# Another rounding of float64 weights, and seven block products for every batch of the second token product

## The chip, the cores and the metric

The kernel runs on one core of a Trainium2 chip. The metric is the device time of one execution in microseconds (us). A core has several engines, each with its own queue of instructions that it works off in order: TensorE (PE in the profile) multiplies matrices into PSUM banks, VectorE (DVE) works element by element, ScalarE (ACT) applies functions and copies, GpSimd (POOL) can add and issues the accumulating DMAs, and SyncE (SP) issues most of the other DMAs. The engines wait for each other through semaphores.

## The reference

Attention with a hash comes first, and a two-layer mixer over tokens and channels follows. The batch is 4, with 8 heads, 768 tokens and a head width of 64, so the model width is 512.

```python
mask = q_bucket[:, :, :, None] == k_bucket[:, :, None, :]      # 6 sign bits of q @ proj, k @ proj
scores = np.where(mask, scale * np.matmul(q, k.transpose(0, 1, 3, 2)), -1000000000.0)
attn = np.exp(scores - np.max(scores, axis=-1, keepdims=True))
attn = attn / (np.sum(attn, axis=-1, keepdims=True) + 1e-09)
x = np.matmul(attn, v)                                         # (4, 768, 512) after the bridge
h = np.maximum(x.transpose(0, 2, 1) @ w_tok1, 0.0) @ w_tok2    # 768 -> 256 -> 768 over tokens
u = x + h.transpose(0, 2, 1)
h2 = np.maximum(u @ w_ch1, 0.0) @ w_ch2                        # 512 -> 1536 -> 512 over channels
out = (u + h2).astype(np.float32)
```

The four weights arrive as float64, the rest as float32. The kernel computes in float32, so it rounds the weights to float32 on the chip.

## The kernel before

There are three stages, each with an order of instructions that is written out by hand.

**Attention** (`attention`) runs over 16 pairs of heads. A round multiplies keys by queries into PSUM (L345), takes the exponential on ACT (L352), adds the exponentials up on DVE (L379 to L386), multiplies them by the values (L397) and divides. The quotient uses the sums of the pair before: ACT takes a logarithm and an exponential (L425, L426), DVE improves the reciprocal (`newton`, L434 and L436), and ACT copies it to other partitions (L442). The result goes to `XT`, in which features lie on partitions and tokens in the rows.

**Conversion** (class `Conversion`) rounds the weights, 768 numbers to each partition at a time. There are 20 such pieces: twelve for `w_tok1`, `w_tok2` and `w_ch1`, spread over the rounds of attention, and eight for `w_ch2` in the token stage. A float64 is two 32-bit words, `lo` and `hi`. `fetch` issues the load on SP (L168). `begin` shifts the high word by three places and puts sign and top bit back (L179, L182). `join` takes the exponent alone as the unit (L194), scales the low word by it (L198) and adds (L199). `end` squares the high word on ACT (L211), so as to set numbers that are too small to zero, and writes the result (L212). `turnover` and `slot` call these steps: in one call of `slot` the last steps of one piece stand ahead of the first steps of the next. In the token stage three raw buffers are used in turn.

**Tokens** (`tokens`) goes over the four batches. `mix1(b)` multiplies by `w_tok1` (L641, 24 records of a matmul for a batch) and applies relu on ACT (L648) into `r1`; after each of its two blocks it runs one entry of a list of jobs. The list's first entry forms sums of channel weights on DVE (L745 to L750), the others are `slot`. `mix2(b, m)` multiplies by `w_tok2` for one half `m` of the features. For batch 0 it makes four blocks of the product with two matmuls each (L690), which ACT copies (L694). For the other batches it makes seven block products in the way of Strassen and Winograd (L698): ACT copies partial results (L703, L706, L708, L710) and five adds make the four blocks (L713 to L717); the second of them (L714) is done by POOL for batches 1 and 2 and by DVE for batch 3. This needs sums of blocks of the left side (`left_sums`, L664 to L667) and of `w_tok2` (`weight_sums`, L618 to L621). A profile counts each of these float32 matmuls as two records. The blocks go to one of three staging places in turn, and POOL adds them to `XT` in memory by an accumulating DMA (`store`, L681). The stage's order: `mix1(b)`, `left_sums(b)`, then both halves of `mix2(b - 1, ...)` with one job between them; `weight_sums` follows in the round of batch 1. At its end stand both halves of batch 3, with sums for the next stage (`inputs`, L594 and L595) between them. Eight PSUM banks are used in turn.

**Channels** (`channels`) multiplies by `w_ch1` and `w_ch2` with nested block products (nearly all of it at L782). It makes up about half of the time.

A second branch recomputes everything in a careful way if a flag is set; with these inputs it isn't entered.

Of the kernel before, what the change touches and what calls it, by code (L numbers as in the profile page):

```python
# [48 lines left out]
def kernel(  # L49
# [83 lines left out]

    NW = 768

    LEAST = float.fromhex("0x1.2p-15")
    double = w_tok1.dtype == I64
    NE = 2 if double else 1

    class Conversion:  # L140


        def __init__(self, pool, parts, bufs, apart=False):
            self.pool, self.bufs, self.apart = pool, bufs, apart
            self.todo = [
                (w, dst, rows, j, n)
                for w, dst, rows, blocks in parts
                for j in range(*blocks, rows)
                for n in range(0, dst.shape[2], NW // rows)
            ]  # L150
            self.fetched, self.begun, self.ready = [], None, None
            for _ in range(bufs - 1):
                self.fetch()
# [17 lines left out]
        def begin(self):  # L171
            if not self.fetched:
                return
            raw, to, rows = self.fetched.pop(0)
            hi = raw[:, :, 1]
            tmp = self.pool.tile([P, 2, NW], F32, name="tmp", tag="cvt", bufs=1)
            big = tmp[:, 0].bitcast(U32)

            nc.vector.tensor_scalar(  # L179
                big, hi, 3, 0x3FFFFFFF, op0=ALU.logical_shift_left, op1=ALU.bitwise_and,  # L180
            )
            nc.vector.scalar_tensor_tensor(  # L182
                big, hi, 0xC0000000, big, op0=ALU.bitwise_and, op1=ALU.bitwise_or,
            )
            self.begun = raw, tmp, to, rows

        def join(self):
            if not self.begun:
                return
            raw, tmp, to, rows = self.begun  # L190
            self.begun = None
            lo, hi = raw[:, :, 0], raw[:, :, 1].bitcast(F32)
            big, unit = tmp[:, 0], tmp[:, 1]
            nc.vector.tensor_scalar(  # L194
                unit.bitcast(U32), big.bitcast(U32), 0xFF800000, None, op0=ALU.bitwise_and,
            )

            nc.vector.scalar_tensor_tensor(unit, lo, 2.0**-52, unit, op0=ALU.mult, op1=ALU.mult)  # L198
            nc.vector.tensor_tensor(big, big, unit, op=ALU.add)  # L199
            self.ready = hi, big, to, rows  # L200

        def end(self):

            if not self.ready:
                return
            size, big, to, rows = self.ready
            self.ready = None
            hi = size
            if self.apart:
                size = self.pool.tile([P, NW], F32, name="size", tag="size", bufs=1)  # L210
            nc.scalar.activation(size, hi, ACT.Square)  # L211
            nc.vector.scalar_tensor_tensor(  # L212
                to, size.rearrange("p (t n) -> p t n", t=rows), LEAST * LEAST,
                big.rearrange("p (t n) -> p t n", t=rows), op0=ALU.is_ge, op1=ALU.mult,
            )

        def turnover(self):

            self.end()
            self.fetch()  # L220
            self.begin()

        def slot(self):

            self.end()
            self.fetch()
            self.begin()
            self.join()

    pairs = [(b, hp) for b in range(B) for hp in range(NP)]  # L230

# [34 lines left out]
    def attention(pool, psum, W1, W2, x0):  # L266
# [202 lines left out]
        for n in range(len(pairs)):  # L469
            halves = [Half(n, half) for half in range(2)]  # L470
            if n:
                load_v(n + 1)
            for now in halves:
                now.scores()
                if n == now.half == 0:
                    hashes(1)
                now.add()
                if now.half == 0:
                    now.add_last()
            if before:  # L480
                before.sums()
            if 0 < n < len(pairs) - 1:
                hashes(n + 1)
            halves[1].add_last()
            if n == 0:
                load_v(1)
            load_qk(n + 2)
            add_values(n)
            if before:
                before.newton()  # L490
            weights.join()
            halves[0].weigh()
            if n + 1 == len(pairs):
                before.divide()
                before = Quotients(halves)
                before.sums()
                before.newton()
                weights.turnover()
                halves[1].weigh()
                break  # L500
            if before:
                before.divide()
            weights.turnover()
            halves[1].weigh()
            if n and n % 2 == 0:
                bounce(pool.tile([P, 2 * S], F32, name="stage", tag="stage", bufs=1), n - 2)
            if n == 2 * NP:
                fetch(0, x0)
            before = Quotients(halves)
# [90 lines left out]
    def tokens(pool, psum, W1, W2, x0, weights, jobs, T, places):  # L600
# [68 lines left out]
        def mix2(b, m):  # L669

            r1, new = R1[b]
            a00, a01, s1, a11 = (
                r1[:, k, P * (2 * m + i) : P * (2 * m + i) + P] for i in range(2) for k in range(2)
            )
            new = new[:, :, P * m : P * m + P]
            ps = [bank("t2")[:, :HALF] for _ in range(4)]
            to = places[(2 * b + m + 1) % 3].rearrange("p (i n t) -> p i n t", i=2, n=2)
            p1, u, p7, p57 = (to[:, i, n] for i in range(2) for n in range(2))

            def store():  # L680
                nc.gpsimd.dma_start(  # L681
                    out=XT[:, 2 * m : 2 * m + 2, S * b : S * b + S], in_=to.rearrange("p i n t -> p i (n t)"),
                    accum_op=ALU.add,
                )

            if not b:
                for n in range(4):
                    for k in range(NJ):
                        at = P * (2 * m + n // 2)
                        nc.tensor.matmul(  # L690
                            ps[n], r1[:, k, at : at + P], W2[:, k, HALF * (n % 2) : HALF * (n % 2) + HALF],
                            start=(k == 0), stop=(k == NJ - 1),
                        )
                    nc.scalar.copy(to[:, n // 2, n % 2], ps[n])  # L694
                return store()

            def product(at, left, right, start=True):
                nc.tensor.matmul(  # L698
                    ps[at], left, right, start=start, stop=True, skip_group_check=True,
                )  # L700

            product(0, a00, b00)
            nc.scalar.copy(p1, ps[0])  # L703
            product(1, a01, b10)
            product(2, s1, sums[:, 0])
            nc.scalar.copy(p57, ps[2])  # L706
            product(3, new[:, 1], b01)
            nc.scalar.copy(p7, ps[3])  # L708
            product(0, new[:, 0], sums[:, 1], False)
            nc.scalar.copy(u, ps[0])  # L710
            product(2, new[:, 2], b11, False)
            product(3, a11, sums[:, 2], False)
            nc.vector.tensor_tensor(p1, ps[1], p1, op=ALU.add)  # L713
            (nc.gpsimd if b + 1 < B else nc.vector).tensor_tensor(p57, p7, p57, op=ALU.add)  # L714
            nc.vector.tensor_tensor(p57, p57, u, op=ALU.add)  # L715
            nc.vector.tensor_tensor(p7, ps[3], u, op=ALU.add)
            nc.vector.tensor_tensor(u, ps[2], u, op=ALU.add)  # L717
            store()

        for b in range(B):  # L720
            mix1(b)
            if b:
                left_sums(b)
                mix2(b - 1, 0)
                job()
                mix2(b - 1, 1)
            if b == 1:
                weight_sums()
        mix2(B - 1, 0)
        inputs(0, T, 0)  # L730
        mix2(B - 1, 1)
# [639 lines left out]
    def attention_and_tokens(W1, W2, x0):  # L1371
# [11 lines left out]
        second["tile"] = second_tile  # L1383

        def weights(pool):
            return Conversion(pool, [(w_ch2, WC2, 3, (0, NHT))], bufs=3, apart=True)

        def jobs(conversion):
            early, late = weight_sums(
                WC1, SW1, slice(0, NCB // 2), slice(NCB // 2, NCB), slice(0, DCH // 2), slice(DCH // 2, DCH),  # L1390
            )
            return [
                lambda: (early(), late()),
                *[conversion.slot] * (NHT * DM // NW + 1),
            ]

        SW2 = second["SW2"].rearrange("p i k c -> p i (k c)")
# [3 lines left out]
    def careful_attention_and_tokens(W1, W2, x0):  # L1401
        def weights(pool, psum):
            conversion = Conversion(pool, [(w_tok1, W1, 3, (0, NR)), (w_tok2, W2, 1, (0, NJ))], bufs=3)
            while conversion.fetched or conversion.ready:
                conversion.slot()

        def turned(pool, psum):
            turn(0, x0, lambda: psum.tile([P, 2, 512], F32, name="trp", tag="tr", bufs=2))
# [58 lines left out]
```

## Time and profile before

Three executions took 805.69, 806.47 and 807.1 us. The profiled one took 806.47 us and has a span of 804.6 us from its first to its last instruction.

| stage | from (us) | to (us) |
|---|---|---|
| start-up and first round of attention | 0 | 27.3 |
| attention, other rounds | 27.3 | 315.65 |
| tokens | 315.65 | 397.24 |
| channels | 397.24 | 795.55 |
| last sums and stores | 795.55 | 804.6 |

Lines such as "L698" point into the kernel before. In a group of instructions "out<-in" are the program's names for what is written and read (`t` is a PSUM bank of the token stage, `second` is memory that holds the staging places and, beside them, converted `w_ch2`, `raw` a loaded float64 piece, `tmp` its working space), followed by the shapes and the count. Durations are in nanoseconds in groups and in microseconds in the time line. A wait names the instruction that waited, then, behind an arrow, the one that ended last before it went on.

### The profile page before, as it was taken

How to read it: one execution, taken by the hardware profiler on the slowest of the kernel's cores; microseconds unless marked ns; L12 is line 12 of the kernel's file. 1: busy time of each engine (PE TensorE's matmuls, PEld its weight loads, DVE VectorE, ACT ScalarE, POOL GpSimd, SP SyncE). 2: the span in 40 equal slices, each digit the busy share in tenths (PEclk: the TensorE clock that was granted, in tenths of full speed). 3: DMA queues.
4: the chain of work that ended last, by engine and by line, in shares of the span. 5: the costliest groups of instructions: out<-in, count | busy, mean ns of one | idle time of the engine just before them, and what ended most of it. 6: DMA issues, size and time to landing. Idle time of an engine off the chain costs nothing.

```text
span 804.6 us, 10632 instructions
## 1 busy us (share of the span) xinstructions
PE 794.9 (99%) x3889; PEld 471.3 (59%) x3889; DVE 672.2 (84%) x884; ACT 441.2 (55%) x707; POOL 57.4 (7%) x80
## 2 busy tenths in 40 slices
PE   9999999999999999999999999999999999999996
PEld 5444444444444444454444458876667886666885
DVE  4789999999999677989867879888769897778986
ACT  5688888888888886243223221237773335775111
POOL 1000000000000000022221010011100012000000
PEclk9999999999999999999999999999999999999999
DMA  4435353537353424886646995499744578630454
GB/s 162 158 121 159 121 160 122 160 121 238 130 165 107 140 61 159 236 248 171 153 79 206 302 355 196 159 282 270 243 141 140 216 211 198 213 110 1 159 180 114
DMA packets 90701, 138.09 MB, mean 172 GB/s; under 512 B 29640, under 2 KB 63376, under 8 KB 88336
## 3 DMA queue, kind: packets, MB, share of 16 engines
q1 hardware_dynamic: 82480, 112.47, 41.9%
q0 software_dynamic: 7456, 24.12, 13.3%
q10 hardware_dynamic: 704, 0.74, 0.3%
q8 instruction: 33, 0.54, 0.3%
q14 instruction: 28, 0.23, 0.1%
HBM read 97.21 MB, written 33.16 MB: 162 GB/s over the span
## 4 chain that ended last, share of the span: by engine, by line
PE 95%; DVE 3%; issue 1%; POOL 0%; ACT 0%; DVEq 0%; POOLq 0%
PE b L782 49%; PE sc L345 20%; PE acc L397 16%; PE t L641 4%; PE sums L421 2%; PE t L690 1%; PE hp L306 1%; PE t L698 1%; PE hw L324 1%; PE idle L459 0%; DVE tmp L179 0%; DVE second L713 0%; DVE second L715 0%; POOL second L714 0%; DVE second L212 0%
## 5 line engine op out<-in xcount | busy, mean ns | idle before, releaser
L352 ACT ACTIVATE e<-sc 128x768 f32<-128x768 f32 x192 | 154.0, 810 | 12.8 <-PE sc L345 12.5
L345 PE MATMUL sc<-qk 64*128 64x384 f32 x768 | 156.7, 487 | 0.0
L782 PE MATMUL b<-R,second 128*128 128x256 f32 (+1 forms) x612 | 150.9, 404 | 0.0
L782 PEld LDWEIGHTS b<-R,second 128*128 128x128 f32 x612 | 116.3, 190 | 31.6 <-issue 17.2
L788 ACT COPY c<-b 128x512 f32<-128x512 f32 (+1 forms) x78 | 37.4, 488 | 169.5 <-PE b L782 155.7
L397 PE MATMUL acc<-e,vn 128*64 128x384 f32 x768 | 127.6, 488 | 0.0
L383 DVE TENSOR_TENSOR esd<-esd,e 128x768 f32<-128x768 f32 x96 | 92.0, 958 | 10.0
L397 PEld LDWEIGHTS acc<-e,vn 128*64 128x64 f32 x768 | 53.6, 137 | 73.1 <-issue 71.8
L345 PEld LDWEIGHTS sc<-qk 64*128 64x128 f32 x768 | 67.5, 187 | 49.3 <-issue 46.4
L782 PE MATMUL b<-XT,WC 128*128 128x256 f32 (+1 forms) x264 | 82.6, 457 | 0.1
L782 PEld LDWEIGHTS b<-XT,WC 128*128 128x128 f32 x264 | 50.1, 190 | 30.1 <-issue 25.1
L345 PE MATMUL sc<-bits 64*128 64x384 bf16 x384 | 62.9, 323 | 0.2 <-DVE bits L328 0.2
L379 DVE SCALAR_TENSOR_TENSOR esd<-e 128x768 f32<-128x768 f32 x32 | 30.3, 948 | 17.6 <-ACT e L352 17.6
L641 PE MATMUL t<-x,W 128*128 128x512 f32 x96 | 41.8, 593 | 0.0
L442 ACT COPY rec<-rec 32x384 f32<-32x384 f32 x64 | 32.6, 509 | 10.1 <-DVE rec L436 9.5
L681 POOL DMA_DIRECT2D XT<-second x8 | 9.9, 1235 | 382.9 <-DVE tmp L198 338.3
L782 PE MATMUL b<-XT,SW 128*128 128x256 f32 (+1 forms) x120 | 34.6, 422 | 0.0
L345 PEld LDWEIGHTS <-bits 64*128 64x128 bf16 x384 | 19.3, 94 | 25.4 <-DVE bits L328 0.8
L782 PE MATMUL b<-TA,WC 128*128 128x512 f32 x72 | 33.8, 592 | 0.0
L782 PE MATMUL b<-TA,SW 128*128 128x512 f32 x72 | 32.9, 592 | 0.0
L403 ACT ACTIVATE num<-acc,vsum 128x384 f32<-128x384 f32 x32 | 18.6, 581 | 24.9 <-PE acc L397 24.5
L386 DVE TENSOR_TENSOR esd<-esd,e 128x768 f32<-128x768 f32 x32 | 30.5, 954 | 1.9
(220 smaller groups left out, 1149.8 us busy)
## 6 DMA issues: line engine op xcount, KB each, us to landing
second<-left SPq DMA_DIRECT2D x18, 1344.0 KB
raw<-in_moe_w_ch SPq DMA_DIRECT2D x16, 768.0 KB
qk<-in_qk SPq DMA_DIRECT2D x15, 768.0 KB
seen<-in_qk POOLq DMA_DIRECT2D x21, 384.0 KB, 3.9
WC<-hidden_left SPq DMA_DIRECT2D x15, 448.0 KB
vn<-in_v SPq DMA_DIRECT2D x16, 384.0 KB
vt<-in_vT SPq DMA_DIRECT2D x16, 384.0 KB
x<-bounced SPq DMA_DIRECT2D x4, 1536.0 KB
```

Source lines behind the costliest of these rows:

```text
L345: nc.tensor.matmul(sc[:, i, :HALF], t[rows, 1, P * c : P * c + P], t[rows, 0, qs], start=start, stop=not start,)
L352: nc.scalar.activation(e, sc[:, :, :HALF], ACT.Exp, scale=SCALE)
L379: nc.vector.scalar_tensor_tensor(self.d, es[0], NR * EPS, es[1], op0=ALU.add, op1=ALU.add,)
L383: nc.vector.tensor_tensor(self.d, self.d, e, op=ALU.add)
L386: nc.vector.tensor_tensor(self.d, self.d, self.es[-1], op=ALU.add)
L397: nc.tensor.matmul(acc[D * i : D * i + D], vn[:, i, c], e[:, i], start=(c == 0), stop=(c == NR - 1),)
L403: nc.scalar.activation(nums[self.n][:, self.half], acc, ACT.Identity, scale=-1.0, bias=vsum,)
L421: nc.tensor.matmul(ps[at : at + 32], ones[:, :32], self.halves[h].d[:, i], start=True, stop=True,)
L442: nc.scalar.copy(rec[other : other + 32, h], rec[at : at + 32, h])
L641: nc.tensor.matmul(ps, W1[:, r, P * j : P * j + P], x[:, r], start=(r == 0), stop=(r == NR - 1),)
L782: nc.tensor.matmul(ps, left(k), right(k), start=start and k == ks[0], stop=stop and k == ks[-1], skip_group_check=True,)
L788: nc.scalar.copy(c, ps)
```

## The change

It has two parts.

*Rounding.* ACT now multiplies the high word, read as a float32, by 2 to the power of minus 112 and takes its absolute value into a buffer `size`; this step is `begin`, and it takes over what the square was for. `join` takes the shifted exponent as the unit, shifts `size` itself in place, scales the low word and adds. `end` puts the sign of the high word back. In attention `begin` moves from `turnover` to the place ahead of `newton`, so a piece is now begun and ended in the same round. In tokens a job is `one`: begin, join, end and fetch of one piece. There is a `size` buffer for each raw buffer but one (one in attention, two in tokens) and one `unit` buffer, in place of `tmp`.

*Second token product.* Batch 0 is now also made by seven block products. So `weight_sums` moves to batch 0's round, ahead of `left_sums`, which now runs for batch 0 too. All five adds are on DVE for every batch.

```diff
         def begin(self):
...
-            hi = raw[:, :, 1]
-            tmp = self.pool.tile([P, 2, NW], F32, name="tmp", tag="cvt", bufs=1)
-            big = tmp[:, 0].bitcast(U32)
-
-            nc.vector.tensor_scalar(
-                big, hi, 3, 0x3FFFFFFF, op0=ALU.logical_shift_left, op1=ALU.bitwise_and,
-            )
-            nc.vector.scalar_tensor_tensor(
-                big, hi, 0xC0000000, big, op0=ALU.bitwise_and, op1=ALU.bitwise_or,
-            )
-            self.begun = raw, tmp, to, rows
+            size = self.pool.tile([P, NW], F32, name="size", tag="size", bufs=self.bufs - 1)
+            nc.scalar.activation(size, raw[:, :, 1].bitcast(F32), ACT.Abs, scale=EXPONENTS)
+            self.begun = raw, size, to, rows
 
         def join(self):
...
             nc.vector.tensor_scalar(
-                unit.bitcast(U32), big.bitcast(U32), 0xFF800000, None, op0=ALU.bitwise_and,
+                unit.bitcast(U32), size.bitcast(U32), 3, 0x7F800000,
+                op0=ALU.logical_shift_left, op1=ALU.bitwise_and,
             )
-
-            nc.vector.scalar_tensor_tensor(unit, lo, 2.0**-52, unit, op0=ALU.mult, op1=ALU.mult)
-            nc.vector.tensor_tensor(big, big, unit, op=ALU.add)
-            self.ready = hi, big, to, rows
+            nc.vector.tensor_scalar(
+                size.bitcast(U32), size.bitcast(U32), 3, None, op0=ALU.logical_shift_left,
+            )
+
+            nc.vector.scalar_tensor_tensor(unit, raw[:, :, 0], 2.0**-52, unit, op0=ALU.mult, op1=ALU.mult)
+            nc.vector.tensor_tensor(size, size, unit, op=ALU.add)
+            self.ready = raw, size, to, rows
 
         def end(self):
...
-            nc.scalar.activation(size, hi, ACT.Square)
             nc.vector.scalar_tensor_tensor(
-                to, size.rearrange("p (t n) -> p t n", t=rows), LEAST * LEAST,
-                big.rearrange("p (t n) -> p t n", t=rows), op0=ALU.is_ge, op1=ALU.mult,
+                to.bitcast(U32), hi, 0x80000000, size, op0=ALU.bitwise_and, op1=ALU.bitwise_or,
             )
...
+        def one(self):
+
             self.begin()
-
-        def slot(self):
-
+            self.join()
             self.end()
             self.fetch()
-            self.begin()
-            self.join()
...
             add_values(n)
+            weights.begin()
             if before:
                 before.newton()
             weights.join()
...
-            if not b:
-                for n in range(4):
-                    for k in range(NJ):
...
-                    nc.scalar.copy(to[:, n // 2, n % 2], ps[n])
-                return store()
-
...
-            (nc.gpsimd if b + 1 < B else nc.vector).tensor_tensor(p57, p7, p57, op=ALU.add)
+            nc.vector.tensor_tensor(p57, p7, p57, op=ALU.add)
...
         for b in range(B):
             mix1(b)
+            if b == 0:
+                weight_sums()
+            left_sums(b)
             if b:
-                left_sums(b)
                 mix2(b - 1, 0)
                 job()
                 mix2(b - 1, 1)
-            if b == 1:
-                weight_sums()
...
-                *[conversion.slot] * (NHT * DM // NW + 1),
+                *[conversion.one] * (NHT * DM // NW),
```

More of the change, by code (lines that the diff above doesn't have):

```diff
@@ L134 @@
     NW = 768
-    LEAST = float.fromhex("0x1.2p-15")
+    EXPONENTS = 2.0**-112
     double = w_tok1.dtype == I64
@@ L140, with __init__ @@
     class Conversion:
-        def __init__(self, pool, parts, bufs, apart=False):
-            self.pool, self.bufs, self.apart = pool, bufs, apart
+        def __init__(self, pool, parts, bufs):
+            self.pool, self.bufs = pool, bufs
             self.todo = [
@@ L189, in join @@
                 return
-            raw, tmp, to, rows = self.begun
+            raw, size, to, rows = self.begun
             self.begun = None
-            lo, hi = raw[:, :, 0], raw[:, :, 1].bitcast(F32)
-            big, unit = tmp[:, 0], tmp[:, 1]
+            unit = self.pool.tile([P, NW], F32, name="unit", tag="unit", bufs=1)
             nc.vector.tensor_scalar(
-                unit.bitcast(U32), big.bitcast(U32), 0xFF800000, None, op0=ALU.bitwise_and,
-            )
-            nc.vector.scalar_tensor_tensor(unit, lo, 2.0**-52, unit, op0=ALU.mult, op1=ALU.mult)
-            nc.vector.tensor_tensor(big, big, unit, op=ALU.add)
-            self.ready = hi, big, to, rows
+                unit.bitcast(U32), size.bitcast(U32), 3, 0x7F800000,
+                op0=ALU.logical_shift_left, op1=ALU.bitwise_and,
+            )
+            nc.vector.tensor_scalar(
[4 more added lines that the diff above has]
+            self.ready = raw, size, to, rows
         def end(self):
@@ L205, in end @@
                 return
-            size, big, to, rows = self.ready
+            raw, size, to, rows = self.ready
             self.ready = None
-            hi = size
-            if self.apart:
-                size = self.pool.tile([P, NW], F32, name="size", tag="size", bufs=1)
-            nc.scalar.activation(size, hi, ACT.Square)
+            hi, size = (a.rearrange("p (t n) -> p t n", t=rows) for a in (raw[:, :, 1], size.bitcast(U32)))
             nc.vector.scalar_tensor_tensor(
-                to, size.rearrange("p (t n) -> p t n", t=rows), LEAST * LEAST,
-                big.rearrange("p (t n) -> p t n", t=rows), op0=ALU.is_ge, op1=ALU.mult,
+                to.bitcast(U32), hi, 0x80000000, size, op0=ALU.bitwise_and, op1=ALU.bitwise_or,
             )
@@ L678, in mix2 @@
             p1, u, p7, p57 = (to[:, i, n] for i in range(2) for n in range(2))
[L680 to L684, printed above, removed]
-            if not b:
-                for n in range(4):
-                    for k in range(NJ):
[L689 to L693, printed above, removed]
-                    nc.scalar.copy(to[:, n // 2, n % 2], ps[n])
-                return store()
             def product(at, left, right, start=True):
@@ L717, in mix2 @@
             nc.vector.tensor_tensor(u, ps[2], u, op=ALU.add)
-            store()
+            nc.gpsimd.dma_start(
+                out=XT[:, 2 * m : 2 * m + 2, S * b : S * b + S], in_=to.rearrange("p i n t -> p i (n t)"),
+                accum_op=ALU.add,
+            )
         for b in range(B):
             mix1(b)
+            if b == 0:
+                weight_sums()
+            left_sums(b)
             if b:
-                left_sums(b)
                 mix2(b - 1, 0)
@@ L1385, in weights @@
         def weights(pool):
-            return Conversion(pool, [(w_ch2, WC2, 3, (0, NHT))], bufs=3, apart=True)
+            return Conversion(pool, [(w_ch2, WC2, 3, (0, NHT))], bufs=3)
         def jobs(conversion):
@@ L1403, in weights @@
             conversion = Conversion(pool, [(w_tok1, W1, 3, (0, NR)), (w_tok2, W2, 1, (0, NJ))], bufs=3)
-            while conversion.fetched or conversion.ready:
-                conversion.slot()
+            while conversion.fetched:
+                conversion.one()
         def turned(pool, psum):
```

## The prediction

> **What bounds the kernel now.** I read the page first, then the chain of waits in order of time, the busy time by stage, the waits of TensorE, and last the time line of the one stage that the change touches.
>
> ```profile
> span 804.6 us, 10632 instructions
> ...
> PE 794.9 (99%) x3889; PEld 471.3 (59%) x3889; DVE 672.2 (84%) x884; ACT 441.2 (55%) x707; POOL 57.4 (7%) x80
> ...
> PE 95%; DVE 3%; issue 1%; POOL 0%; ACT 0%; DVEq 0%; POOLq 0%
> ```
>
> TensorE (PE) is 99% busy and 95% of the chain that ended last. A faster VectorE (DVE) is worth nothing where PE has no gap. So the question is where PE's gaps are. By stage (columns: stretch, its length, busy us of PE, weight loads, DVE, ScalarE (ACT), GpSimd (POOL), then clock and DMA; the stretches are start-up, attention, its end, tokens, channels, tail):
>
> ```profile
> 0.00:27.30 27.30, 26.13 (x162) 13.27 (x162) 14.38 (x20) 12.50 (x17) 3.33 (x20) 1.00 0.49 175
> 27.30:306.12 278.82, 278.82 (x1980) 134.25 (x1984) 245.61 (x301) 233.58 (x346) 0.00 (x0) 1.00 0.42 136
> 306.12:315.65 9.53, 9.53 (x64) 3.51 (x64) 6.91 (x10) 6.68 (x14) 0.00 (x0) 1.00 0.72 248
> 315.65:397.24 81.59, 79.51 (x215) 39.92 (x213) 72.09 (x96) 28.09 (x53) 12.27 (x10) 1.00 0.74 202
> 397.24:795.55 398.31, 398.31 (x1466) 278.43 (x1467) 329.70 (x449) 160.01 (x278) 41.76 (x50) 1.00 0.63 190
> 795.55:804.60 9.05, 2.56 (x12) 1.90 (x10) 3.55 (x10) 0.37 (x1) 0.00 (x0) 0.80 0.22 67
> ```
>
> Attention and channels have no PE gap at all, although DVE is at 88% and 83% there. Only the token stage has one, 2.08 us. The waits of PE and of ACT name it:
>
> ```profile
> PE t L698 <- ACT second L703: 1.9, 1, 1.9
> ...
> ACT second L703 <- DMA XT<-second: 4.7, 1, 4.7
> ```
>
> The time line shows how it comes about (start, length, engine, line; in brackets the idle time before and its releaser):
>
> ```profile
> 387.40 0.55 DVE L713 TENSOR_TENSOR second<-t,second 128x384 f32<-128x384 f32 x1
> 387.90 1.21 POOL L681 DMA_DIRECT2D XT<-second  x1 [6.99 <-DVE second L717]
> ...
> 394.39 0.48 ACT L703 COPY second<-t 128x384 f32<-128x384 f32 x1 [4.72 <-DMA XT<-second]
> ...
> 394.92 0.91 PE L698 MATMUL t<-W2sums,r1s 128*128 128x384 f32 x2 [1.90 <-ACT second L703]
> ...
> 396.63 0.55 DVE L713 TENSOR_TENSOR second<-t,second 128x384 f32<-128x384 f32 x1
> ...
> 397.24 0.30 PEld L782 LDWEIGHTS b<-XT,WC 128*128 128x128 f32 x2 [0.73 <-DVE second L713]
> ```
>
> DVE lags behind PE. It ends batch 2's first half product at 387.5, though the last matmul for it ended at 381.3. The accumulating store then lands about 6.4 us after its issue, and frees the staging place for batch 3's second half: PE stands 1.9 us. At the end the channel stage's first weight load waits 0.73 us for a late DVE add.
>
> **What the skill says.** "VectorE: DVE Perf Modes", The perf-mode tier table: fp32 tensor_scalar from SBUF runs at 2x, tensor_tensor at 1x. The trace agrees, also for the two-operation form and for a strided source: 0.56 against 0.96 us for 768 elements. "SBUF — State Buffer", Who interferes with whom: a DVE instruction in a 2-port mode, or with two SBUF inputs, and a GpSimd instruction exclude each other in full. The trace agrees: beside the POOL add of 369.41 the tensor_scalar took 2.12 us. "ScalarE: Activation LUTs", Table sets: abs is in every table set, like relu and copy. The trace shows one table load (1.28 us) in the whole run, though relu, copy, square, exp and ln are all used; it has no Abs.
>
> **The change part by part.**
>
> ```profile
> L179 DVE TENSOR_SCALAR tmp<-raw x20: 552/560/2120, 25.1 to 377.8; 128x768 uint32<-128x768 uint32 x20
> L182 DVE SCALAR_TENSOR_TENSOR tmp<-raw,tmp x20: 957/959/972, 25.7 to 378.5; 128x768 uint32<-128x768 uint32 x20
> L198 DVE SCALAR_TENSOR_TENSOR tmp<-raw,tmp x20: 957/959/1678, 42.6 to 380.1; 128x768 f32<-128x768 uint32 x20
> ```
>
> *Conversions, 20 of them.* Before: two tensor_scalars, three scalar_tensor_tensors and an add, on start-to-start distances of 0.59+0.99+0.60+0.99+1.0+0.99 = 5.2 us of DVE, and one Square of 0.92 us. After: two tensor_scalars, two scalar_tensor_tensors (the strided high word of the last costs nothing more, see L182) and an add: 4.2 us; ACT's Square becomes an Abs of the same form, 0.92. So 1.0 us of DVE less for each. Twelve lie in attention (12 us of DVE, worth 0: PE has no gap). In an attention round the Abs moves ahead of the copies of the reciprocals, where ACT waited 0.5 us at 137.7 for DVE; the Square behind them goes. Those copies move some 0.3 us, and the pause before the last num (1.35 us) takes that up. The eight in tokens save 8 us of DVE.
>
> *Batch 0's product.* The chain prices it:
>
> ```profile
> 336.52 10.32 PE t L690 x32
> ...
> 357.14 9.04 PE t L698 x28
> ```
>
> Sixteen matmuls become fourteen: PE -1.28 us, and in a stage bound by PE that is time. DVE gets four left sums (1.8 us) and twice five adds (2.65 each): +7.1. ACT keeps eight copies.
>
> *Adds from POOL to DVE.* Four POOL adds (mean 1.42 us) become DVE adds of 0.55: +2.2 us. In return DVE is no longer held: L179 1.56 too long at 369, L194 0.69 at 361, L198 0.72 at 380, and a plain wait of 2.2 at 390: -5.2.
>
> Sum on DVE in tokens: -8 + 7.1 + 2.2 - 5.2 = -3.9 us. The early stages of the queue get more, the late ones less, so I laid the new order on the old starts (weight_sums 2.1 us now ahead of batch 1):
>
> - DVE: first conversion 327.7 to 331.9, weight sums to 334.0, left sums of batch 0 to 335.8; conversions to 340.0 and 344.2; left sums 1 to 346.0; batch 0's adds to 348.7 and, after a conversion, from 352.9 to 355.5; two conversions to 363.9; left sums 2 to 365.7; batch 1's adds to 368.4 and, after a conversion, to 375.2; last conversion to 379.4; left sums 3 to 381.2; batch 2's adds to 383.9 and 386.5; batch 3's first to 389.9.
> - PE without a wait: batch 0's halves from 336.4 and 340.9, mix1(2) 345.4, batch 1's 355.7 and 360.2, mix1(3) 364.7, batch 2's 375.0 and 379.5, batch 3's 384.05 and 388.55, end 393.1.
>
> Each need of PE is met: left sums 0 (335.8 for 336.4, the tightest), left sums 1 to 3 by 3 to 10 us, each PSUM bank that a DVE add frees by over 1 us (tightest: batch 2's add of ps2 for batch 3). The store of batch 2's first half is issued at about 384.3 instead of 387.9, lands at 390.7, and the copy behind it ends at 391.1, when the fifth product of the last half is due (388.55 + 4 x 0.645 = 391.1). The 1.9 us gap closes, or almost. The last half's first add ends by 392.8, before PE, so the 0.73 goes too.
>
> *New waits.* Each conversion's first DVE instruction now waits for its Abs, which stands in ACT's queue behind a relu or a copy that waits for PE; before, the Square stood there and the last DVE instruction waited. Behind the DVE instruction wait the left sums and adds above; their starts already contain it. The Abs in turn waits for its size buffer (two in tokens), that is for the conversion two before, and for raw data. Closest are the fourth (340.0 for 340.3) and the seventh (359.7 for 360); behind them stand mix2's copies, which PE needs some 2 us later. Raw loads get 7 us or more; in the old run a load issued at 332.82 was over by 336, when DMA falls to 88 GB/s for 4 us. On SP the load of x for batch 3 stands behind a raw load that now goes at 340.1 instead of 338.0; it is needed at 364.7. I put all this at 0.
>
> **Sum**: -1.28 - 1.9 - 0.73 = -3.9, and some 0.1 of small semaphore gaps: -4.0 us on the span of 804.6. The channel stage is shifted whole: its first stores and sums come earlier by about as much. The profiled run took 806.47, which is also the median of the three (805.69 to 807.1), so 802.5. What cannot be told from no change is about 0.2%, 1.6 us.
>
> **Rivals.**
> - *Tight waits bite* (0.15): left sums 0, the store or a size buffer come 0.5 to 1.5 us late once or twice. Gain 1.7 to 3, time about 804.2. For: three margins under 0.7 us. Against: the sum of DVE work falls.
> - *PE's gap only moves* (0.07): the store or DVE's longer queue after batch 0 keeps PE waiting as long as now, and only the two matmuls are won: -1.3 or less, 805.2 to 806.5. For: DVE stays near 90% busy.
> - *Slower through ACT* (0.07): Abs isn't in the loaded set, so each conversion costs two loads, 2.57 us, in ACT's queue. An attention round has about 1.35 us of pause before the last num and three score banks as slack; beyond that PE stops, about 1 us in 12 rounds, and about 2 us each at three mix2 copies: +18 - 4, about 820. It decides from some 1.4 us more of ACT per round. Against: the skill's sentence. A late size buffer would show as the same wait; it needs 5.6 us of lag for slower.
> - The change does less than it says: not possible for the matmuls, which are fixed counts.
>
> **Chances.** Main case 0.71 (own range 801.6 to 803.4). Faster by over 0.2%: 0.71 + 0.15 = 0.86, less 0.02 for noise: 0.84; within: 0.08; slower: 0.08. The upper end takes in the tight waits; the lower is the whole gap (-4.3) and the spread of the runs: 801.3 to 805.2.
>
> **What would show it.** In the profile after: t by L698's successor with 112 matmul records and none by the old four-product loop; 20 Abs of about 0.92 us and one table load; no POOL add on this staging; token stage about 77.6 us; PE's wait for the copy under 0.5 us; channels still 398.3. Wrong would be: a PE wait for left sums at the first half product, a wait of PE for copies that stand behind an Abs, or a second table load.

## The result and the profile after

The changed kernel takes 803.19 us (median of six, 802.61 to 805.62) against 806.56 us for the kernel before (median of six beside it). The ratio is 0.9959 with a 95% interval of 0.9941 to 0.9978, that is 3.3 us less, between 1.8 and 4.8. The forecast was 802.5 us, in a range of 801.3 to 805.2. A second comparison, told of below, gave 0.9945 (0.9931 to 0.9958).

From here on an "L" number in a view points into the kernel that the view is of. The page of the changed kernel has the same bound as before: TensorE is 99% busy, and it now makes up 98% of the chain that ended last instead of 95%.

```profile
span 801.7 us, 10590 instructions
...
PE 793.3 (99%) x3885; PEld 470.8 (59%) x3885; DVE 659.1 (82%) x882; ACT 441.6 (55%) x707; POOL 52.4 (7%) x76
...
PE 98%; DVE 1%; issue 0%; ACT 0%; DVEq 0%
```

Busy time by stage, with the columns of the prediction's table (start-up, attention, its end, tokens, channels, tail):

```profile
0.00:27.68 27.68, 26.51 (x162) 13.28 (x162) 14.95 (x22) 13.32 (x18) 3.34 (x20) 1.00 0.48 170
27.68:306.50 278.82, 278.82 (x1980) 134.25 (x1984) 233.53 (x288) 232.72 (x345) 0.00 (x0) 1.00 0.42 137
306.50:316.03 9.53, 9.53 (x64) 3.51 (x65) 6.92 (x10) 6.68 (x14) 0.00 (x0) 1.00 0.72 248
316.03:394.26 78.23, 77.69 (x210) 39.54 (x209) 70.52 (x107) 28.32 (x53) 7.42 (x6) 1.00 0.76 210
394.26:792.50 398.24, 398.24 (x1468) 278.34 (x1467) 329.93 (x448) 160.22 (x279) 41.64 (x50) 1.00 0.62 191
792.50:801.70 9.20, 2.52 (x12) 1.89 (x10) 3.27 (x9) 0.34 (x1) 0.00 (x0) 0.82 0.22 66
```

Attention lasts 278.82 us to the hundredth as before, though VectorE works 12.1 us less in it (245.61 to 233.53). Tokens fall from 81.59 to 78.23 us, 3.36 less. Channels and tail are unchanged within 0.2 us. Start-up is 0.38 us longer in this execution. The span falls by 2.9 us: 3.36 won in the token stage, less 0.38 in start-up and 0.08 in channels and tail.

The chain in order of time has the matmuls of batch 0's product (start, length):

```profile
336.90 9.03 PE t L674 x28
```

It took 10.32 us before: 1.29 us saved. The waits of TensorE and the time line show what became of the gap:

```profile
PE t L674 <- ACT second L679: 0.5, 1, 0.5
```

```profile
381.12 0.56 DVE L693 TENSOR_TENSOR second<-t,second 128x384 f32<-128x384 f32 x1
...
381.66 0.64 SPq L1024 DMA_DIRECT2D left<-second  x1
...
382.10 1.21 POOL L694 DMA_DIRECT2D XT<-second  x1 [7.12 <-DVE second L693]
...
391.69 0.48 ACT L679 COPY second<-t 128x384 f32<-128x384 f32 x1 [3.36 <-PE t L674]
...
392.22 0.91 PE L674 MATMUL t<-W2sums,r1s 128*128 128x384 f32 x2 [0.54 <-ACT second L679]
...
394.26 3.60 PE L761 MATMUL b<-XT,WC 128*128 128x512 f32 x8
```

VectorE now ends batch 2's first half product at 381.7 instead of 387.5. The store goes out at 382.1, but the copy that needs its staging place starts only at 391.69, 9.6 us later. The profile names TensorE as the releaser of that copy, but the matmul had been done nearly 2 us before (in the last experiment the same copy starts 1.9 us earlier in the stage, 0.2 us after its matmul). The store is what it waited for. It is the slowest of its kind in this kernel (from issue to landing, minimum, median and maximum of eight):

```profile
DMA to landing us min/median/max: 6.3/6.9/9.5
```

So 0.54 us of the 1.90 stay. The wait of 0.73 us at the start of channels is gone. 1.29 + 1.36 + 0.73 = 3.38, and the stage fell by 3.36.

### The profile page after: what moved, and what is told of

It is laid out like the page before. It is cut to its first block, busy times and chain, and to the rows that moved or that the text cites. A ratio compares the mean times of both kernels' runs of the same rounds, so it can differ in the third digit from the quotient of the medians.

```text
span 801.7 us, 10590 instructions
## 1 busy us (share of the span) xinstructions
PE 793.3 (99%) x3885; PEld 470.8 (59%) x3885; DVE 659.1 (82%) x882; ACT 441.6 (55%) x707; POOL 52.4 (7%) x76
## 4 chain that ended last, share of the span: by engine, by line
PE 98%; DVE 1%; issue 0%; ACT 0%; DVEq 0%
PE b L761 49%; PE sc L337 20%; PE acc L389 16%; PE t L634 5%; PE t L674 5%; PE sums L413 2%; PE hp L298 1%; PE hw L316 1%; PE idle L451 0%; DVE second L1196 0%; DVE R L1155 0%; DVE R L1152 0%; DVE q L1182 0%; DVE second L1182 0%; DVE bits L318 0%
```

## The experiments

All ratios below are to the kernel before on the same chip. "Token stage" is from the first matmul of `mix1(0)` to the first of channels in the profiled execution; it leaves out the start-up, which varies by some microseconds from one execution to the next (last section). Theory A is the prediction's: VectorE's lag in the token stage makes TensorE's gap, and attention is indifferent to VectorE.

| kernel | ratio (95% interval) | token stage (us) | TensorE's wait in it (us) |
|---|---|---|---|
| before | 1 | 81.59 | 1.9, and 0.7 at its end |
| changed | 0.9959 (0.9941 to 0.9978) | 78.23 | 0.5 |
| rounding alone | 0.9959 (0.9943 to 0.9974) | 79.12 | none listed |
| product alone | 1.0034 (1.0022 to 1.0046) | 84.86 | 6.4 |
| product alone, square in place | 1.0041 (1.0029 to 1.0053) | 85.05 | 4.6 |
| POOL keeps its adds | 0.9973 (0.9964 to 0.9983) | 79.35 | 1.7 |
| one size buffer | 0.9985 (0.9978 to 0.9993) | 80.63 | 2.0 |
| unused adds in tokens | 1.0078 (1.0058 to 1.0098) | 85.75 | 6.2 |
| unused adds in attention | 0.9960 (0.9945 to 0.9975) | 78.45 | 0.8 |
| Abs three times in attention | 0.9986 (0.9978 to 0.9994) | 78.24 | 0.6 |
| residuals later | 0.9948 (0.9929 to 0.9966) | 77.43 | none |
| weight store later | 0.9937 (0.9921 to 0.9952) | 77.42 | none |

### Each part alone

For the rounding alone, `mix2` and the order of the sums are those of the kernel before, and POOL does its adds:

```diff
-            if b == 0:
-                weight_sums()
-            left_sums(b)
             if b:
+                left_sums(b)
                 mix2(b - 1, 0)
                 job()
                 mix2(b - 1, 1)
+            if b == 1:
+                weight_sums()
```

> Only the rounding is changed; batch 0 keeps its four blocks with two matmuls each, the weight sums stay in batch 1's round and POOL keeps its adds. Theory A (VectorE's lag in the token stage makes TensorE's gap): eight pieces at 1.0 us less bring batch 2's adds forward by several us, the store goes out early enough, and both the 1.9 us gap and the 0.73 us at the start of channels go: about -2.6 us against the kernel before, 804.0 us, with a token stage of 79.0 us. Rival B (the gap is made by the stores, which follow each other one at a time, whatever VectorE does): 0 to -0.7 us. Rival C (the gain comes from attention, where 12 us of VectorE are saved): a shorter round of attention than 19.21 us.

It took 804.62 us, 0.9959. The token stage of 79.12 us against the 79.0 of theory A is 2.5 us less than before, with a VectorE that is busy 65.3 us in it instead of 72.1 (the stage's row, then the store of batch 2's first half):

```profile
316.21:395.33 79.12, 78.98 (x214) 40.30 (x213) 65.26 (x89) 28.25 (x53) 11.61 (x10) 1.00 0.75 207
```

```profile
384.36 1.21 POOL L674 DMA_DIRECT2D XT<-second  x1 [3.15 <-DVE second L710]
```

A round of attention is still 19.21 us, so rival C falls. Rival B falls too: fewer instructions on VectorE alone brought this store from 387.90 to 384.36, and the stage came down with it.

For the product alone, class `Conversion` and its calls are those of the kernel before, the rest is as changed:

```diff
-            size = self.pool.tile([P, NW], F32, name="size", tag="size", bufs=self.bufs - 1)
-            nc.scalar.activation(size, raw[:, :, 1].bitcast(F32), ACT.Abs, scale=EXPONENTS)
+            tmp = self.pool.tile([P, 2, NW], F32, name="tmp", tag="cvt", bufs=1)
+            big = tmp[:, 0].bitcast(U32)
...
-                *[conversion.one] * (NHT * DM // NW),
+                *[conversion.slot] * (NHT * DM // NW + 1),
```

> Only the second token product is changed (seven block products for batch 0, weight sums earlier, all adds on VectorE); the old rounding stays. Theory A: TensorE has 1.28 us less to do, but VectorE gets 7.1 us for batch 0 and 2.2 us for the adds, and gets back only some 3 us of contention and 2.6 us of idle time before batch 2's adds. These come about 3 us later than before, left sums of batch 3 too (about 388.5 for TensorE's 384), and TensorE waits 4 to 7 us: 2 to 4 us slower than the kernel before, about 809.5 us. Rival B: -1.3 us, 805.2.

It took 810.14 us, 1.0034, so 2.7 us more than before although TensorE has 1.3 us less to do. The size is what theory A said; the way is partly another. Not the left sums stop TensorE, but ScalarE (waits of the product-alone kernel in its token stage, then its time line):

```profile
ACT size L211 <- DVE second L212: 9.0, 4, 2.6
...
PE t L681 <- ACT second L686: 6.4, 4, 2.0
```

```profile
381.02 0.91 ACT L211 ACTIVATE size<-raw 128x768 f32<-128x768 f32 x1 [2.64 <-DVE second L212]
...
382.36 0.91 PE L681 MATMUL t<-W2sums,TA 128*128 128x384 f32 x2 [2.02 <-ACT second L686]
```

The old square writes to a single buffer that VectorE's last step of the piece before still reads. Late on VectorE, that step holds the square, and behind the square in ScalarE's queue stand the copies that free PSUM for TensorE. Three of the four gaps (1.83, 0.49 and 2.02 us) are of this kind, the last (2.02 us) is the store. The next experiment takes that buffer away by squaring in place, as the old kernel does in attention:

```diff
-            return Conversion(pool, [(w_ch2, WC2, 3, (0, NHT))], bufs=3, apart=True)
+            return Conversion(pool, [(w_ch2, WC2, 3, (0, NHT))], bufs=3)
```

> The kernel with the product alone (old rounding), with the square written over the raw high word also in the token stage, as in attention, so that there is no single size buffer for ScalarE to wait for. In the product-alone kernel TensorE stood 4.3 us at three places behind ScalarE's wait for that buffer, and 2.0 us behind batch 2's store. If those three gaps are the cause of its slowness, it becomes 4 us faster (about 806). If VectorE's load is, the gaps only move: VectorE is busy 78.9 of 84.9 us, batch 2's store still goes out at about 391 and lands at 397.6, and TensorE waits there for 6 us instead of 2: within 0.7 us of the product-alone kernel, 809.7. I expect the second.

It took 810.72 us, 1.0041: no faster, as the second reading said, though not in the way it said, since TensorE waits only 0.3 us at the store instead of 6. It isn't a clean test of the buffer, though: ScalarE now waits for the first steps of the same piece, which read the raw word (10.3 us in all), so gaps of the first kind came back in another form (2.16 and 1.40 us the longest). What both kernels share is VectorE's load: it is busy 78.9 of 84.9 us in the one and 79.1 of 85.1 in the other, and batch 2's store leaves 75.7 and 75.9 us after the start of the stage, against 72.3 before and 66.1 in the changed kernel. That the load is the cause, and the order of ScalarE's queue only the place where it shows, is the likelier reading; these two kernels alone don't prove it. The unused adds of the next section load VectorE in another way and also lengthen the stage.

So the parts don't add up. Product alone costs 2.7 us and rounding alone saves 3.3; together they save 3.3. By the times, then, nothing is seen of what the product adds to the rounding. By the token stages it is 0.9 us (79.12 to 78.23): roughly the 1.3 us of the two matmuls, less the gap of 0.54 us that came back. The product gains only where the rounding has made room on VectorE.

### More and less work on VectorE

One add whose result isn't used goes behind the last add of `join`, once in attention's pieces (`bufs == 2`) and once in those of the token stage (`bufs == 3`):

```diff
             nc.vector.tensor_tensor(size, size, unit, op=ALU.add)
+            if self.bufs == 2:
+                nc.vector.tensor_tensor(unit, size, unit, op=ALU.add)
```

> The changed kernel with one more VectorE add of 768 elements (0.96 us, its result isn't used) in each of the twelve pieces converted in attention, which gives back what the new rounding saves there. Theory A: attention has no TensorE gap, so 11.5 us of VectorE cost nothing: the changed kernel's time within 0.3 us, and rounds of 19.21 us. Rival C (attention profits from the saving): 1 to 10 us slower.

> The changed kernel with the same unused add in each of the eight pieces converted in the token stage. Theory A: VectorE is busy without a break there, so batch 2's adds and batch 3's left sums come up to 7 us later, and TensorE waits: first about 0.3 us for left sums of batch 0's successor pieces, then for left sums of batch 3 (379 + 7 = 386 for TensorE's 384) and for the store (lands about 395 for 391): 4 to 6 us slower than the changed kernel, 808. Rival B (the stores alone set the gap): same as the changed kernel within 0.5 us.

In attention it cost nothing: 804.10 us, 0.9960. In tokens, 813.00 us, 1.0078: the token stage is 7.5 us longer than the changed kernel's for eight times 0.96 us. That is more than the 4 to 6 us expected; VectorE's lag passes to TensorE almost whole, at the store (2.4 us), at a copy behind a late Abs (0.9), at a bank that a late add frees (0.7), and at the start of channels (2.2). The left sums of batch 3, which were expected to be late, are not among these (waits of TensorE in that stage):

```profile
PE t L676 <- ACT second L681: 3.3, 2, 2.4
...
PE b L763 <- DVE second L695: 2.2, 1, 2.2
...
PE t L676 <- DVE second L694: 0.7, 1, 0.7
```

The timed executions grew by more (9.6 us by the ratios, each with an interval of some 1.6 us either way; the profiled execution was the shortest of the six); what the rest is, the trace doesn't show.

### POOL's adds

```diff
-            nc.vector.tensor_tensor(p57, p7, p57, op=ALU.add)
+            (nc.gpsimd if b + 1 < B else nc.vector).tensor_tensor(p57, p7, p57, op=ALU.add)
```

> The changed kernel with the second add of batches 0 to 2 given back to POOL. Theory A: VectorE saves 0.55 us on each of six adds and pays again for contention and for waits on POOL, 0.7 to 2.2 us each; batch 2's first store goes out 1 to 2 us later and TensorE's gap grows from 0.54 to about 2 us: 1 to 2 us slower than the changed kernel, 804.7. Rival D (POOL's adds were free, VectorE just has fewer to do): same as the changed kernel or 0.5 us faster.

It took 804.48 us, 0.9973, about 1.1 us slower than the changed kernel. The two intervals overlap, but the token stage, 1.12 us longer, agrees. VectorE is busy 72.7 us in it instead of 70.5, with six adds fewer to do: it is held while POOL adds. The store left 68.5 us after the start of the stage instead of 66.1.

```profile
PE t L674 <- ACT second L679: 1.7, 1, 1.7
```

The prediction's sentence on who is held was too wide for VectorE instructions with two SBUF inputs: the page "SBUF — State Buffer" of the Trainium skill, Who interferes with whom, says that these contend with a GpSimd instruction that reads SBUF, not with one that only writes it. POOL's add reads it, and the kernel before shows such a case, an L198 of 1.68 us instead of 0.96 beside the add of 379.92, so the prices stand.

### The size buffers

```diff
-            size = self.pool.tile([P, NW], F32, name="size", tag="size", bufs=self.bufs - 1)
+            size = self.pool.tile([P, NW], F32, name="size", tag="size", bufs=1)
```

> The changed kernel with one size buffer in the token stage instead of two. Theory G (a late size buffer holds Abs in ScalarE's queue, and with it the copies that TensorE waits for, as the Square did in the kernel with the product alone): the third Abs waits for the second piece's end, from 337.4 to 339.7, the later ones likewise; VectorE in turn waits 1 us for each Abs. TensorE gaps of 1 to 2 us at two to four half products: 4 to 8 us slower than the changed kernel, 807 to 811. If the second buffer is idle luxury: same within 0.5 us.

It took 805.84 us, 0.9985: 2.1 us slower than the changed kernel by the ratios, 2.4 in the token stage. The mechanism is the one expected, the size about half of the least that was expected (4 to 8 us):

```profile
339.77 0.89 ACT L177 ACTIVATE size<-raw 128x768 f32<-128x768 f32 x1 [2.21 <-DVE second L206]
...
341.08 0.91 PE L674 MATMUL t<-W2sums,TA 128*128 128x384 f32 x2 [1.58 <-ACT second L679]
```

The Abs waited at 337.6 to 339.8, as worked out, four times in all (7.0 us), but only the first of these held TensorE for long; before the others the copies had more time. TensorE's listed waits grew by 1.5 us (0.5 to 2.0); the rest of the 2.4 doesn't appear as a wait. So the second buffer is part of the gain.

### ScalarE's slack in attention

Abs is issued three times in each of attention's twelve rounds, in place of a second table load:

```diff
-            nc.scalar.activation(size, raw[:, :, 1].bitcast(F32), ACT.Abs, scale=EXPONENTS)
+            for _ in range(3 if self.bufs == 2 else 1):
+                nc.scalar.activation(size, raw[:, :, 1].bitcast(F32), ACT.Abs, scale=EXPONENTS)
```

> The changed kernel with each Abs in attention done three times, 1.84 us more of ScalarE in each of twelve rounds; it stands for the slower rival of the prediction, in which table loads would have cost 2.57 us each. The prediction put ScalarE's slack at about 1.35 us in a round, the pause before the last num, and three score banks beyond that. If the pause is all the slack: 0.5 us in each of twelve rounds, 6 us slower than the changed kernel, 809.5, with rounds of 19.7 us. If the banks take up the rest: rounds stay at 19.21 us and the time is the changed kernel's, 803.5.

It took 805.89 us, 0.9986, some 2.2 us slower than the changed kernel, between the two expectations. Most rounds remain at 19.21 us; five are longer by 0.3 to 0.6 us, 2.6 us in all, and these are the cause. Half of that is listed as a wait of TensorE for the copy of the numerators out of a score bank:

```profile
PE sc L338 <- ACT num L396: 1.3, 4, 0.3
```

So 1.84 us a round is just past ScalarE's slack. One Abs in place of one Square is far from it. The changed kernel has one table load in the whole run (1.28 us), so the rival of two loads for each piece did not come about.

### What makes the store slow

In the changed kernel, a weight store of 768 KB leaves SP at 381.66, 0.4 us ahead of batch 2's store, and three residual copies of 512 KB before it, since 373.5. The last of these copies waits until the store of batch 1's second half has landed, and the weight store follows it, 0.4 us after that landing (383.8 and 384.18 before, 381.3 and 381.66 changed). So a VectorE that is quicker with batch 2 brings its store up to the weight store. The first edit issues the residuals later; the weight store, no longer behind them in SP's queue, then leaves at 351.5. The second leaves the residuals and issues only the weight store later:

```diff
-            if t == 1:
+            if t == 3:
                 residual(0)
```

> The changed kernel with the copy of the first residuals from XT to the output issued two steps later in the channel stage (after t = 3 begins instead of t = 1). Theory E (the 0.54 us gap that is left comes from batch 2's first store landing 9.6 us after its issue instead of 6.4, since the residual copies and a weight store run beside it): the store lands after about 6.5 us and the gap goes: 0.5 us faster than the changed kernel, 802.7. Rival F (the store is slow because of something else, such as the raw weights or the store before it): landing stays above 9 us and the gap at 0.5.

```diff
-                [], sums, [whole("p1"), second_parts("p7")], *([second_parts(name)] for name in ("p6", "p3", "p5", "p2", "p4")),
+                [], sums, [second_parts("p7")], [second_parts("p6"), whole("p1")], *([second_parts(name)] for name in ("p3", "p5", "p2", "p4")),
```

> The changed kernel with the 768 KB store of channel weights p1 issued one step later, behind the other weight sums; the residual copies stay where they are. It parts the two neighbours of batch 2's first store. If the weight store slows it: landing after about 6.5 us, no TensorE gap, 0.5 us faster than the changed kernel. If the residual copies do: landing stays at about 9 us and the gap at about 0.5 us; same as the changed kernel. I expect the first, since the weight store is issued at 381.7, 0.4 us ahead of the store, and the last residual copy at 381.

Both close the gap: token stages of 77.43 and 77.42 us, with TensorE busy for the whole of it. The second parts the two neighbours. Its residual copies leave SP as before, and the store is no longer slow (time line of the kernel with the later weight store):

```profile
380.90 1.21 POOL L694 DMA_DIRECT2D XT<-second  x1 [7.07 <-DVE second L693]
...
388.57 0.48 ACT L679 COPY second<-t 128x384 f32<-128x384 f32 x1 [1.46 <-PE t L674]
```

The copy behind the store starts as soon as its matmul is done, 0.2 us after it, so the store had landed within 7.7 us. By its own record it took 7.4 us (7.5 with the later residuals), against 9.5 in the changed kernel and 6.4 before. So the weight store made some 2 us of the 3 by which the store had slowed, and the residuals none that shows. Both expectations of 6.5 us were missed: what makes the last 1 us stays open, though TensorE doesn't wait for it.

The other kernels' traces show how near the weight store has to be. Where it left SP 3.3 to 3.7 us ahead of batch 2's store, that store took 6.4 or 6.5 us (before, product alone, square in place); 1.8 us ahead, 6.9 (unused adds in tokens); 1.5 us ahead, 8.2 and 8.3 (POOL keeps its adds, rounding alone); 0.4 us ahead, 9.4 or 9.5 (changed, one size buffer, and the two with more work in attention). These kernels differ in other things too, so this is a pattern, and the later weight store is the test of it.

The later weight store has the lowest median seen, 802.24 us or 0.9937. Its distance to the changed kernel was measured once more with both on one chip:

> The changed kernel once more, on the same chip as the next kernel. Ratio to the kernel before 0.996, token stage 78.2 us, a TensorE gap of about 0.5 us.

> The changed kernel with the later weight store, once more beside the changed kernel itself. If the 0.5 us of gap and the 0.3 us of small waits around it are all that the move is worth, it is 0.8 us faster than the changed kernel (ratio to before 0.995), with a token stage of 77.4 us and no gap. If the first comparison's 1.8 us were real, the rest would have to show outside of the token stage.

They took 802.78 us (0.9945) and 802.55 us (0.9943, 0.993 to 0.9957). The token stages are 78.27 and 77.43 us. So the 0.84 us are plain in the traces, and the times alone don't part the two kernels; the 1.8 us by which the first ratios differed did not come again.

## Why the prediction was right, and where it was off

**Where PE's gaps are.** Right. All that was won lies in the token stage. The 12 us of VectorE saved in attention moved nothing, which the unused adds confirm, and the channel stage is as long as before. "Only the token stage has one" left out the start-up (1.2 us) and the tail (6.5 us), which the change doesn't touch.

**Two matmuls.** Right: 1.28 forecast, 1.29 in the chain.

**Conversions.** Right in kind. The three lines of the new steps (minimum, median and maximum in ns) are as the nearest old rows had them:

```profile
L177 ACT ACTIVATE size<-raw x20: 903/918/937, 21.4 to 371.0; 128x768 f32<-128x768 f32 x20
L187 DVE TENSOR_SCALAR unit<-size x20: 549/560/561, 25.5 to 373.2; 128x768 uint32<-128x768 uint32 x20
L206 DVE SCALAR_TENSOR_TENSOR second<-raw,size x8: 957/957/959, 331.1 to 376.3; 128x768 uint32<-128x768 uint32 x8
```

One piece took 3.9 us from start to start (328.07 to 332.00 for the first), not 4.2: the distance between the second tensor_scalar and the next instruction is 0.47 us, where I had put 0.6 from the old order, and from the last step to what follows it is 0.88, where I had put 0.99. Over eight pieces VectorE came 2 us earlier than laid out, and batch 2's adds ended at 381.7 where 383.9 was forecast. The maximum of 2.12 us beside POOL's add is gone as well. The sum on VectorE held: of the 3.9 us less that were forecast, 2.2 were a wait for POOL and not busy time, which leaves 1.7; its busy time fell from 72.09 to 70.52.

**The tight margins.** All held but one. Left sums of batch 0 ended at 335.8 for a matmul at 336.7, the fourth Abs began at 340.54 straight behind the copies, the seventh at 359.87. The size experiment shows that this margin was real: with one buffer less it breaks.

**The store.** This is the term that was mis-sized. I took 6.4 us from issue to landing, what this store took before and also the median of the eight, though another of them took 11.2. Now it took 9.5. An earlier store met a weight store that hadn't been so near before: 387.90 against 384.18 then, 382.10 against 381.66 now. The two errors hang together: the store left 2 us sooner than forecast, which brought it close behind the weight store, and what it won by leaving it lost in landing (391.6 against the forecast 390.7). So the error came out as 0.54 us of gap instead of none. This is the first rival ("tight waits bite") in its smallest form, added to the main case. By the token stage, 3.36 us against the 4.0 forecast.

**The rivals.** That the gap only moves was wrong for this kernel, and right for the product alone. The slower rival's place (ScalarE's queue) was well chosen: late size buffers there do stop TensorE, as two experiments show. Its price for attention was too high: by its own count of slack, 1.84 us more in each of twelve rounds would have cost 6 us, and 2.2 were measured. The 2.57 us of two table loads were not tried.

## What to carry to other kernels

A change that looks like less work for the busiest engine (here two matmuls) can lose on another engine's queue: ask what it adds there, and whether that queue has room in that stage. Work that is removed from an engine is worth something only in a stretch in which someone waits for it; 12 us were worth nothing in attention. In tokens 8 us less won 2.5 us, nearly all of the 2.6 us of waiting there was, and 7.7 us more cost 7.5. When a step is brought forward, look up which transfers will now be its neighbours; a median landing time from the old place doesn't hold there.

## What the runs showed of the hardware that I had not expected

The second half of the first load of queries and keys lands at times that differ by over 2 us between executions of the same start. TensorE's wait for it is none in the kernel before, 0.4 us in one repetition of the changed kernel and 0.7 with the rounding alone. In the kernel with unused adds in attention, whose token stage starts at 318.79 us instead of 316.03, it is this:

```profile
PE hw L318 <- DMA qk<-in_qk: 2.4, 1, 2.4
```

Among kernels whose rounds of attention were all 19.21 us the token stage began between 314.82 us (later weight store) and that 318.79. This wait is 2.4 us of the spread; the rest also lies in the start-up, and its cause was not traced. The spread is as large as the whole effect of the change. A stage is better compared from its own start than by the span.
